# The fourth attention pair's last four chunks transposed two a turn, in a fused attention and two-MLP kernel

## The chip, the cores and the metric

The kernel runs on one core of a Trainium2 chip. The metric is the device time of one execution in microseconds. Three timed executions of the kernel before took 1118.45, 1120.15 and 1120.5 us; their median is 1120.15 us. One more execution was profiled, and all rows below come from it.

## The reference

```python
def _attn_ref(q, k, v, tau):                  # 4 batches, 8 heads, 576 rows, 64 wide
    scores = scale * np.matmul(q, k.transpose(0, 1, 3, 2))
    thresh = np.max(scores, axis=-1, keepdims=True) - tau
    scores = np.where(scores >= thresh, scores, -1000000000.0)
    scores = scores - np.max(scores, axis=-1, keepdims=True)
    attn = np.exp(scores)
    attn = attn / (np.sum(attn, axis=-1, keepdims=True) + 1e-09)
    return np.matmul(attn, v)

def _moe_ref(x, w_in, w_out, s, b):           # 2304 tokens, 512 -> 2048 -> 512
    r = np.maximum(x @ w_in, 0.0)
    return (s * (r * r) + b) @ w_out

def _moe2_ref(x, w_in, w_out):
    h = x @ w_in
    return (h * np.tanh(softplus(h))) @ w_out
...
```

Attention's output, 2304 tokens of 512, goes through the first MLP and then through the second.

## The kernel before

**Attention** goes by pairs of heads: 16 pairs, numbered from 0, four to a batch, so pair 3 is the fourth and completes the first batch. A pair has nine score tiles of 128 rows and nine chunks of 128 key columns. The generator `attention` runs in turns. Turn `k` writes out the scores of pair `k // 9`, tile `k % 9`: TensorE computes `S` (line 346), VectorE scales it into `ns` and takes its maximum (350), ScalarE takes the exponential `e` (358), VectorE masks and sums it (364), and GpSimd normalises it (374). The same turn writes out chunk `k - 7` (`LAG = 7`): `weights_t` transposes the chunk's five blocks into the PSUM tile `T` (387, 392), and ScalarE copies that to `te` (398). `T` has one buffer, so each transposing waits for the copy of the chunk before it. When chunk 6 of a pair has been copied, `products_v` multiplies chunks 1, 4 and 0 by v into `pv` (414, 417), 12 matmuls; after chunk 8 it does chunks 3 and 2, 8 matmuls (two chunks of 64 rows go in as one, and chunk `c` takes `te_c` and `te_(c+5)`). I call these the first and the second run of products. Then `split_x` puts `pv` into the two halves `xh` (ScalarE, 425) and `xl` (VectorE, 426). The scores and the transposes of q and k for later pairs (`tpq`, `tpk`) share the PSUM tile `S`; their copies are `hiq`, `hik` (284) and `loq`, `lok` (285).

**The first MLP** (`moe1`, line 516 is its matmul) takes a batch when the batch's four pairs have their `x`. `run` first advances attention alone, until pair 3 has its `x`; on the turns in `AHEAD` (15, 20, 24, 29, 33, 38, 42) it also takes a step of the loading and splitting of the MLP's weights (lines 62 to 79). From then on it advances attention and MLP in turn, by the nanoseconds that each `yield` names. A third generator, `combine`, prepares the second MLP's weights between them: ScalarE and VectorE operations of lines 105 to 145 on tiles `crawi`, `afi`, `chli`, and stores to `wsi` (147).

**The order** in which this is written out isn't the order on the engines. A scheduler places each instruction by its own model of when operands and buffers are ready; what was written out earlier goes first where several are ready, attention ahead of the MLP. `issue_after` binds one instruction behind another: the first transpose of a turn behind the run of products written out in that turn. Each engine then works its queue strictly in that order, SyncE's queue of DMAs too.

Of the kernel before, what the change touches and what calls it, by code (L numbers as in the profile page):

```python
# [19 lines left out]
class Fused:  # L20
# [131 lines left out]
    def combine_all(self):  # L152
# [3 lines left out]
        def load(i):  # L156
            if i < 16 and i not in raws:
                raws[i] = self.combine_load(*steps[i])

        for i, step in enumerate(steps):  # L160
            if i not in raws:
                load(i)
                yield
                yield
            yield from self.combine(*step, raws.pop(i), lambda: i + 1 != EARLY and load(i + 1))

# [263 lines left out]
    def attention(self):  # L430

        nc = self.nc
        self.turn = 0
        N = 9 * self.B * self.NP
        LAG = 7
        for n in "kq":
            self.load_raw(0, n)
        nc.sync.dma_start(self.tau_c, self.tau.partition_broadcast(P))  # L440
        nc.sync.dma_start(self.s_c, self.s.partition_broadcast(P))
        nc.sync.dma_start(self.b_c, self.b.partition_broadcast(P))
        for pr in range(2):
            self.load_raw(pr, "v")
        warm = self.pvp.tile([P, 1024], F32, tag="pv", name="warm")[:, :512]
        self.busy(warm[:, :256], 20)
        self.prep_first(lambda n: self.busy(warm[:, :256], 2 * n))
        fin = todo = None
        tes = {}
        for k in range(N + LAG + 2):  # L450
            pr, ti = divmod(k, 9)
            self.turn = k
            if k < N:
                nxt = self.scores(pr, ti)
                if k < 12:
                    self.busy(warm[:, :256], 3)
                if fin:
                    fin()
                fin = nxt
                yield 550  # L460
                if pr + 1 == self.B * self.NP and ti == 2:
                    self.load_raw(pr, "v")
                if pr + 1 < self.B * self.NP and ti in (1, 4):
                    self.prep_qk(pr + 1, "kq"[ti // 4])
                    if ti == 4 and pr >= 2:
                        with self.tc.issue_after(self.moved):
                            self.load_raw(pr, "v")
                    yield 500
            elif fin:
                fin()  # L470
                fin = None
            j = k - LAG
            run = None
            if todo:
                tp, tc, te = todo
                tes[tc] = te
                if tc == 6:
                    run = self.products_v(tp, (1, 4, 0), tes, True, False)
                    yield 1460
                elif tc == 8:  # L480
                    run = self.products_v(tp, (3, 2), tes, False, True)
                    yield 970
                    self.split_x(tp)
            todo = None
            if 0 <= j < N:
                prj, ci = divmod(j, 9)
                todo = prj, ci, self.weights_t(prj, ci, run)
                yield 550

    def acc(self, name):  # L490
# [297 lines left out]
    def run(self, ctx):  # L788
# [28 lines left out]
        while 3 not in self.x:  # L817
            next(att)
            if self.turn > done and self.turn in AHEAD:
                next(w1)  # L820
# [13 lines left out]
        def moes():  # L834
# [5 lines left out]
            for b in (1, 2):  # L840
                while 4 * b + 3 not in self.x:
                    yield 0
                for i, c in enumerate(self.moe1(b)):
                    while n * 256 < (2 + 12 * EARLY) * (i + 128 * (b - 1)):
                        next(comb, None)
                        n += 1
                    yield c
            while self.combined < EARLY:
                next(comb)
# [46 lines left out]


EARLY = 14
AHEAD = [15] + [9 * pr + ti for pr in (2, 3, 4) for ti in (2, 6)]
HALVES = [slice(0, 64), slice(64, 128)]  # L900

# [49 lines left out]
```

## Time and profile before

| | |
|---|---|
| timed executions, median (lowest, highest) | 1120.15 us (1118.45, 1120.5) |
| profiled execution, its own time | 1117.13 us |
| its span, first to last instruction | 1114.9 us |
| TensorE matmuls busy | 1073.3 us, 96% |
| weight loads busy | 1012.0 us, 91% |
| VectorE, ScalarE, GpSimd busy | 792.9, 624.9, 285.1 us |
| mean granted TensorE clock | 0.995 of full speed |

A row of the stretch view gives a stretch in us from the span's start, its length, each engine's busy time with the number of instructions, the granted clock, and the DMA engines' share and rate. In the timeline a row is a group of like instructions: start, duration, engine, line, operation, what is written and read; in brackets how long the engine stood idle before it, and what ended that.

### The profile page before, as it was taken

How to read it: one execution, taken by the hardware profiler on the slowest of the kernel's cores; microseconds unless marked ns; L12 is line 12 of the kernel's file. 1: busy time of each engine (PE TensorE's matmuls, PEld its weight loads, DVE VectorE, ACT ScalarE, POOL GpSimd, SP SyncE). 2: the span in 40 equal slices, each digit the busy share in tenths (PEclk: the TensorE clock that was granted, in tenths of full speed). 3: DMA queues.
4: the chain of work that ended last, by engine and by line, in shares of the span. 5: the costliest groups of instructions: out<-in, count | busy, mean ns of one | idle time of the engine just before them, and what ended most of it. 6: DMA issues, size and time to landing. Idle time of an engine off the chain costs nothing.

```text
span 1114.9 us, 21378 instructions
## 1 busy us (share of the span) xinstructions
PE 1073.3 (96%) x7964; PEld 1012.0 (91%) x7964; DVE 792.9 (71%) x1662; ACT 624.9 (56%) x1189; POOL 285.1 (26%) x354
## 2 busy tenths in 40 slices
PE   7987899999999999899999989999999999999998
PEld 6766789999899999879999879999999999999998
DVE  5989699998556777878757656735695468725782
ACT  5777687585486575577746667634453245413451
POOL 4556454355072351344515201100000000000000
PEclk9999999999999999999999999999999999999999
DMA  7577588785666879969855599968998999997783
GB/s 165 132 179 218 149 269 243 237 256 178 196 182 216 259 220 285 306 202 310 305 177 196 184 368 359 357 224 311 349 393 314 364 418 380 342 333 255 261 288 119
DMA packets 141590, 292.69 MB, mean 263 GB/s; under 512 B 52848, under 2 KB 78960, under 8 KB 133168
## 3 DMA queue, kind: packets, MB, share of 16 engines
q1 hardware_dynamic: 127104, 277.93, 74.0%
q10 hardware_dynamic: 14384, 13.40, 4.1%
q8 instruction: 63, 1.03, 0.4%
q14 instruction: 39, 0.32, 0.1%
HBM read 201.85 MB, written 66.58 MB: 241 GB/s over the span
## 4 chain that ended last, share of the span: by engine, by line
PE 70%; DVE 5%; DMA 5%; POOL 2%; issue 2%; ACT 1%; SPq 0%; ACTq 0%; DVEq 0%; POOLq 0%
PE o L761 16%; PE y L516 14%; PE h L516 12%; PE qY L627 7%; PE qX L627 5%; PE qV L627 4%; PE S L346 4%; PE pv L417 3%; PE T L387 3%; DMA wsi<-chli 2%; DMA w<-w 2%; POOL e L374 1%; DMA wso<-chlo 1%; PE pv L414 1%; DVE ns L350 1%
## 5 line engine op out<-in xcount | busy, mean ns | idle before, releaser
L761 PE MATMUL o<-wo,hl 128*128 128x256 f32 x1512 | 177.7, 279 | 0.0
L761 PEld LDWEIGHTS o<-wo,hl 128*128 128x128 f32 x1512 | 177.4, 188 | 0.0
L516 PE MATMUL h<-xh,w 128*128 128x288 f32 x768 | 164.6, 299 | 2.2 <-ACT xh L425 0.7
L516 PE MATMUL y<-gh,w 128*128 128x288 f32 x768 | 164.8, 299 | 1.3 <-DVE y L563 0.8
L374 POOL TENSOR_SCALAR e<-e,st 128x576 f32<-128x576 f32 x128 | 140.5, 1109 | 34.0 <-DVE st L369 24.7
L350 DVE TENSOR_SCALAR_CACHE_REDUCE ns<-S 128x576 f32<-128x576 f32 x144 | 108.0, 752 | 43.9 <-PE S L346 43.0
L358 ACT ACTIVATE e<-ns,st 128x576 f32<-128x576 f32 x128 | 98.9, 775 | 71.1 <-DVE ns L350 67.8
L364 DVE SCALAR_TENSOR_TENSOR e<-ns,st,e 128x576 f32<-128x576 f32 x128 | 114.1, 895 | 26.4 <-ACT e L358 22.9
L516 PEld LDWEIGHTS h<-xh,w 128*128 128x128 f32 x768 | 126.0, 188 | 3.7 <-ACT xh L425 1.2
L516 PEld LDWEIGHTS y<-gh,w 128*128 128x128 f32 x768 | 126.3, 188 | 2.5 <-DVE y L563 1.4
L398 ACT COPY te<-T 128x576 f32<-128x576 f32 x144 | 91.2, 633 | 50.2 <-PE T L392 45.1
L540 POOL TENSOR_TENSOR gl<-rr,gh 128x288 fp32r<-128x288 f32 x96 | 90.3, 952 | 108.9 <-ACT rr L539 107.8
L516 PE MATMUL h<-xl,w 128*128 128x288 f32 x384 | 113.7, 296 | 0.0
L516 PE MATMUL y<-gl,w 128*128 128x288 f32 x384 | 113.4, 295 | 0.0
L346 PE MATMUL S<-KH,Q 128*128 128x288 f32 x320 | 96.2, 318 | 15.7 <-DVE ns L350 7.3
L387 PE MATMUL T<-ident,e 128*128 128x128 f32 x576 | 90.9, 278 | 7.2 <-ACT te L398 5.0
L387 PEld LDWEIGHTS T<-ident,e 128*128 128x128 f32 x576 | 68.0, 142 | 24.2 <-issue 13.6
L346 PE MATMUL S<-KL,Q 128*128 128x288 f32 x320 | 89.9, 297 | 0.0
L627 PE MATMUL qY<-yc,wi 128*128 128x384 f32 x432 | 86.6, 337 | 1.3 <-DVE g L650 1.3
L417 PE MATMUL pv<-te,rawv 128*64 128x288 f32 x576 | 87.8, 423 | 0.0
L346 PEld LDWEIGHTS S<-KH,Q 128*128 128x128 f32 x320 | 60.6, 190 | 21.7 <-DVE ns L350 10.5
L627 PEld LDWEIGHTS qY<-yc,wi 128*128 128x128 f32 x432 | 75.6, 188 | 1.9 <-DVE g L650 1.9
(151 smaller groups left out, 2204.1 us busy)
## 6 DMA issues: line engine op xcount, KB each, us to landing
w<-w SPq DMA_DIRECT2D x96, 512.0 KB, 5.4
wo<-wso SPq DMA_DIRECT2D x42, 1024.0 KB, 7.1
wi<-wsi SPq DMA_DIRECT2D x23, 1024.0 KB, 8.2
wi<-wsi SPq DMA_DIRECT2D x25, 768.0 KB, 8.0
w<-wp SPq DMA_DIRECT2D x32, 512.0 KB, 4.7
wsi<-chli SPq DMA_DIRECT2D x24, 512.0 KB, 4.8
wso<-chlo SPq DMA_DIRECT2D x24, 512.0 KB, 7.1
ycd<-yp SPq DMA_DIRECT2D x14, 768.0 KB, 7.6
```

Source lines behind the costliest of these rows:

```text
L346: self.scored = nc.tensor.matmul(so, Q[:, c0:c0 + 128], kt[:, ks], start=(i == 0), stop=(i == len(terms) - 1)).ins
L350: nc.vector.tensor_scalar(ns.rearrange("p (h n) -> p h n", h=2), sv, -0.125, 3.0e38, op0=ALU.mult, op1=ALU.min, accum_out=nm[:, c1])
L358: nc.scalar.activation(e, ns, AF.Exp, bias=nm[:, c1], scale=-1.0)
L364: nc.vector.scalar_tensor_tensor(e, ns, nthr[:, c1], e, op0=ALU.is_le, op1=ALU.mult, accum_out=sm[:, c1])
L374: nc.gpsimd.tensor_scalar(t, t, rinv[:, j:j + 1], u[:, j:j + 1], op0=ALU.mult, op1=ALU.add)
L387: nc.tensor.transpose(T[:, i * 128:i * 128 + 128], self.es[pr, i, "pair"][:, o:o + 128], self.ident)
L398: nc.scalar.copy(te, T[:, :576])
L417: ins = self.nc.tensor.matmul(*args, **kw).ins
L516: nc.tensor.matmul(acc[:, :n], w[:, wl, c], rhs[c][xl][:, ts], start=(i == 0), stop=(i == 11))
L540: (nc.vector if b == 3 else nc.gpsimd).tensor_tensor(gl[:, ts], r2, gh[:, ts].bitcast(F32), op=ALU.subtract)
L627: self.nc.tensor.matmul(acc, a, b, start=(first and i == 0), stop=(i == n - 1), skip_group_check=True)
L761: nc.tensor.matmul(bank[p][t], hl[:, gl, j, ts], w[:, 2 * (q % 2) + j, wl], start=(old is None and q + j + k == 0), stop=(q + j + k == 6), ...
```

## The change

`due(k)` replaces the fixed lag. It gives chunk `k - 7` as before, except in four turns: turn 39 transposes chunks 32 and 33 (pair 3, chunks 5 and 6), turn 40 chunks 34 and 35 (chunks 7 and 8), turns 41 and 42 none. The runs of products hang on chunks 6 and 8 as before, so they are written out in turns 40 and 41 instead of 41 and 43. Only the first transposing of a turn is bound behind that turn's products. `SOLO = 0` selects the same runs as before for every pair. The `yield`s of the products now name 486 ns for each chunk (1458 and 972 instead of 1460 and 970).

```diff
-        fin = todo = None
-        tes = {}
+        fin, todo, tes = None, [], {}
+        soon = {39: (32, 33), 40: (34, 35), 41: (), 42: ()} if TWO else {}
+
+        def due(k):
+            return soon.get(k, (k - LAG,) if 0 <= k - LAG < N else ())
+
...
-            if todo:
-                tp, tc, te = todo
+            for tp, tc, te in todo:
                 tes[tc] = te
-                if tc == 6:
-                    run = self.products_v(tp, (1, 4, 0), tes, True, False)
-                    yield 1460
-                elif tc == 8:
-                    run = self.products_v(tp, (3, 2), tes, False, True)
-                    yield 970
+                for chunks in RUNS[tp < SOLO].get(tc, ()):
+                    run = self.products_v(tp, chunks, tes, chunks == RUNS[tp < SOLO][min(RUNS[tp < SOLO])][0], tc == 8)
+                    yield 486 * len(chunks)
+                if tc == 8:
                     self.split_x(tp)
-            todo = None
-            if 0 <= j < N:
+            todo = []
+            for j in due(k):
                 prj, ci = divmod(j, 9)
-                todo = prj, ci, self.weights_t(prj, ci, run)
+                todo.append((prj, ci, self.weights_t(prj, ci, run)))
+                run = None
                 yield 550
...
+SOLO = 0
+TWO = True
+RUNS = ({6: [(1, 4, 0)], 8: [(3, 2)]}, {5: [(0, 4)], 6: [(1,)], 7: [(2,)], 8: [(3,)]})
```

What the scheduler makes of it is shown at three places. In the rows, the figure behind a tile's name is its chunk or score tile, and the last figure a running number.

TensorE's queue at the first run of products of pair 3, before:

```order
L392 MATMUL T_6_1354<-ident,E_113 128x128
L346 MATMUL S_8_1463<-KH_120,Q_117 128x288
L346 MATMUL S_8_1463<-KL_122,Q_117 128x288
L346 MATMUL S_8_1463<-KH_120,Q_117 128x288
L346 MATMUL S_8_1463<-KL_122,Q_117 128x288
L414 MATMUL pv_1378<-te_6_1360,rawv_136 64x288
```

and now:

```order
L392 MATMUL T_6_1320<-ident,E_113 128x128
L346 MATMUL S_8_1463<-KH_120,Q_117 128x288
L346 MATMUL S_8_1463<-KL_122,Q_117 128x288
L346 MATMUL S_8_1463<-KH_120,Q_117 128x288
L346 MATMUL S_8_1463<-KL_122,Q_117 128x288
L414 MATMUL pv_1362<-te_6_1326,rawv_136 64x288
```

Nothing moved there; the run stands at the same row of the queue, and everything ahead of it on all five queues is in the old order.

TensorE's queue at the second run of products of pair 3 (`T_0` is the first chunk of pair 4), before:

```order
L346 MATMUL S_1_1508<-KL_129,Q_125 128x288
L414 MATMUL pv_1378<-te_8_1427,rawv_136 64x288
L417 MATMUL pv_1378<-te_3_1262,rawv_136 64x288
L417 MATMUL pv_1378<-te_8_1427,rawv_136 64x288
L417 MATMUL pv_1378<-te_3_1262,rawv_136 64x288
L417 MATMUL pv_1378<-te_7_1397,rawv_136 64x288
L417 MATMUL pv_1378<-te_2_1224,rawv_136 64x288
L417 MATMUL pv_1378<-te_7_1397,rawv_136 64x288
L417 MATMUL pv_1378<-te_2_1224,rawv_136 64x288
L387 MATMUL T_0_1451<-ident,e_0_1208 128x128
```

and now:

```order
L346 MATMUL S_1_1508<-KL_129,Q_125 128x288
L387 MATMUL T_0_1455<-ident,e_0_1208 128x128
L387 MATMUL T_0_1455<-ident,e_1_1234 128x128
L387 MATMUL T_0_1455<-ident,e_2_1272 128x128
L387 MATMUL T_0_1455<-ident,e_3_1309 128x128
L392 MATMUL T_0_1455<-ident,E_113 128x128
L414 MATMUL pv_1362<-te_8_1389,rawv_136 64x288
L417 MATMUL pv_1362<-te_3_1262,rawv_136 64x288
```

The five transposes of `T_0` moved from behind the run to ahead of it. Behind them, the next transposing `T_1` also moved ahead of the MLP's first two `h` matmuls on `xh`. On ScalarE the copy `te_0` moved ahead of `xh`.

VectorE's queue where the second batch's MLP ends and the third's is about to begin (`chli` is the weight combining, `y_3` the MLP's last sums), before:

```order
L145 TENSOR_TENSOR chli_5871<-chli_5871 128x2x256
L563 SCALAR_TENSOR_TENSOR y_3_4178<-y_3_3_0_6575,small,y_3_4178 128x288
L350 TENSOR_SCALAR ns_3_5754,st_5549<-S_3_5749 128x576
L353 TENSOR_SCALAR st_5549<-st_5549,small 128x1
L145 TENSOR_TENSOR chli_5991<-afi_5667,chli_5991 128x2x256
L563 SCALAR_TENSOR_TENSOR y_3_4178<-y_3_3_1_6613,small,y_3_4178 128x288
L364 SCALAR_TENSOR_TENSOR e_3_5757,st_5549<-ns_3_5754,st_5549,e_3_5757 128x576
L350 TENSOR_SCALAR ns_4_5797,st_5549<-S_4_5788 128x576
```

and now:

```order
L564 SCALAR_TENSOR_TENSOR y_2_4164<-y_3_2_1_6528,small,y_2_4164 128x288
L145 TENSOR_TENSOR chli_5973<-afi_5637,chli_5973 128x2x256
L350 TENSOR_SCALAR ns_3_5774,st_5587<-S_3_5769 128x576
L564 SCALAR_TENSOR_TENSOR y_3_4165<-y_3_3_0_6557,small,y_3_4165 128x288
L353 TENSOR_SCALAR st_5587<-st_5587,small 128x1
L364 SCALAR_TENSOR_TENSOR e_3_5777,st_5587<-ns_3_5774,st_5587,e_3_5777 128x576
L564 SCALAR_TENSOR_TENSOR y_3_4165<-y_3_3_1_6595,small,y_3_4165 128x288
L350 TENSOR_SCALAR ns_4_5841,st_5587<-S_4_5832 128x576
```

The last `chli` subtraction moved from behind `ns_3` to ahead of it. On TensorE the eight matmuls of `S_4` there moved from behind the first nine `h` matmuls of the third batch to ahead of them.

Elsewhere TensorE's queue is in the old order up to the second batch's MLP but for three swaps of one or two matmuls. From there to about the end of the third batch's MLP, some 2,150 matmuls, attention's steps stand up to 12 MLP matmuls earlier, for one pair later, and on SyncE's, ScalarE's and VectorE's queues the combining's steps stand a few places off. Behind that the queues agree again but for a few neighbours.

## Rows read from the trace of the kernel before

**Rows 1.** Page, busy time of each engine over the span:

```profile
PE 1073.3 (96%) x7964; PEld 1012.0 (91%) x7964; DVE 792.9 (71%) x1662; ACT 624.9 (56%) x1189; POOL 285.1 (26%) x354
```

**Rows 2.** Stretches of the span; the columns are in the first line:

```profile
core 0: us, PE busy (x) PEld busy (x) DVE busy (x) ACT busy (x) POOL busy (x), PEclk, DMA share, GB/s
0.00:140.00 140.00, 115.87 (x829) 95.85 (x830) 112.95 (x288) 93.56 (x175) 72.40 (x104) 0.98 0.66 170
...
316.00:640.00 324.00, 317.38 (x2425) 293.45 (x2425) 236.11 (x566) 205.96 (x414) 127.79 (x145) 0.99 0.76 240
...
112.62:133.08 20.46, 17.41 (x122) 12.84 (x120) 11.49 (x34) 10.44 (x18) 8.85 (x11) 0.92 0.38 119
```

**Rows 3.** Timeline of TensorE around the two runs of products of pair 3:

```profile
118.33 0.46 PE L414 MATMUL pv<-te,rawv 128*64 128x288 f32 x1 [2.01 <-ACT te L398]
...
126.71 0.46 PE L414 MATMUL pv<-te,rawv 128*64 128x288 f32 x1 [0.59 <-ACT te L398]
...
128.81 0.66 PE L387 MATMUL T<-ident,e 128*128 128x128 f32 x4
...
129.41 0.33 PE L276 MATMUL tpk<-ident,rawk 128*128 128x64 f32 x2
...
130.16 0.51 PE L516 MATMUL h<-xh,wp 128*128 128x288 f32 x2
130.51 0.60 PE L387 MATMUL T<-ident,e 128*128 128x128 f32 x4
...
130.97 0.38 PE L516 MATMUL h<-xl,wp 128*128 128x288 f32 x1
...
131.95 0.66 PE L387 MATMUL T<-ident,e 128*128 128x128 f32 x4 [0.20 <-ACT te L398]
```

**Rows 4.** Timeline of ScalarE in the same stretch:

```profile
117.10 0.65 ACT L71 ACTIVATE wraw<-wraw 128x512 f32<-128x512 f32 x1 [2.22 <-DMA wraw<-in_moe_w_out_dram]
...
126.04 0.62 ACT L398 COPY te<-T 128x576 f32<-128x576 f32 x1
...
128.92 0.64 ACT L425 CAST xh<-pv 128x576 fp32r<-128x576 f32 x1 [1.12 <-PE pv L417]
...
130.39 0.69 ACT L284 CAST hik<-tpk 128x640 fp32r<-128x640 f32 x1
131.26 0.64 ACT L398 COPY te<-T 128x576 f32<-128x576 f32 x1 [0.17 <-PE T L392]
```

**Rows 5.** Timelines of VectorE and GpSimd in the same stretch:

```profile
129.59 0.76 DVE L426 TENSOR_TENSOR xl<-pv,xh 128x576 fp32r<-128x576 f32 x1 [0.47 <-ACT xh L425]
...
121.54 3.23 POOL L374 TENSOR_SCALAR e<-e,st 128x576 f32<-128x576 f32 x4 [0.27 <-DVE st L369]
```

**Rows 6.** Stretches after three long waits of TensorE, columns as in rows 2:

```profile
118.00:124.00 6.00, 5.67 (x32) 3.23 (x33) 3.30 (x10) 1.11 (x3) 2.69 (x5) 0.72 0.28 91
473.00:479.00 6.00, 6.00 (x35) 3.44 (x35) 1.80 (x5) 0.86 (x2) 2.23 (x3) 0.72 0.92 231
653.00:659.00 6.00, 4.09 (x28) 2.77 (x29) 5.90 (x13) 2.70 (x5) 0.00 (x0) 1.00 0.87 302
```

**Rows 7.** Waits of TensorE between 316 and 640 us: total us, times, longest:

```profile
PE S L346 <- DVE loq L285: 1.6, 1, 1.6
PE T L387 <- POOL e L374: 1.5, 1, 1.5
...
PE h L516 <- DVE y L563: 0.6, 1, 0.6
```

**Rows 8.** Timelines of VectorE, ScalarE and TensorE where the third batch's MLP begins:

```profile
463.68 0.75 DVE L350 TENSOR_SCALAR_CACHE_REDUCE ns<-S 128x576 f32<-128x576 f32 x1
...
467.31 0.69 DVE L145 TENSOR_TENSOR chli<-afi,chli 128x512 fp32r<-128x512 f32 x1 [2.62 <-ACT chli L143]
...
466.65 0.62 ACT L143 CAST chli<-afi 128x512 fp32r<-128x512 f32 x1 [3.02 <-DMA wsi<-chli]
...
469.89 0.44 PE L276 MATMUL tpq<-ident,rawq 128*128 128x64 f32 x2
```

More of the change, by code (lines that the diff above doesn't have):

```diff
@@ L471, in attention @@
                 fin = None
-            j = k - LAG
             run = None
-            if todo:
-                tp, tc, te = todo
+            for tp, tc, te in todo:
                 tes[tc] = te
-                if tc == 6:
-                    run = self.products_v(tp, (1, 4, 0), tes, True, False)
-                    yield 1460
-                elif tc == 8:
-                    run = self.products_v(tp, (3, 2), tes, False, True)
-                    yield 970
+                for chunks in RUNS[tp < SOLO].get(tc, ()):
+                    run = self.products_v(tp, chunks, tes, chunks == RUNS[tp < SOLO][min(RUNS[tp < SOLO])][0], tc == 8)
+                    yield 486 * len(chunks)
+                if tc == 8:
                     self.split_x(tp)
-            todo = None
-            if 0 <= j < N:
+            todo = []
+            for j in due(k):
                 prj, ci = divmod(j, 9)
-                todo = prj, ci, self.weights_t(prj, ci, run)
+                todo.append((prj, ci, self.weights_t(prj, ci, run)))
+                run = None
                 yield 550
```

## The prediction

> **What bounds the kernel now.** I read the page's busy times first. TensorE's matmuls fill 1073.3 of 1114.9 us [rows 1], so what an edit can win is TensorE's idle time and the time that it runs at a lower clock; the number of matmuls stays the same here. The stretch view then says where that time is [rows 2]. In the first 140 us TensorE is busy for 115.87 us, so 24.1 of its 41.6 idle us lie there, with attention alone at work for most of it. Between 316 and 640 us, where attention and the MLP of the second and third batch are mixed, it idles 324 - 317.38 = 6.6 us. The place of the edit is the stretch from 112.62 to 133.08 us, the end of the attention-only part: TensorE idles 20.46 - 17.41 = 3.05 us there.
>
> The timeline of that stretch names the waits [rows 3]. The first run of products of pair 3 waits 2.01 us for `te_6`, the second 0.59 us for `te_8`, and a later transposing, `T_2` of pair 4, waits 0.20 us for `te_1`. ScalarE's rows tell why `te_6` is late: it stands behind a scaling of weights that itself waits 2.22 us for a load [rows 4]. The clock is the last view. In the six microseconds that begin with the first run it averages 0.72 of full speed [rows 6], so some of them ran at 1.2 GHz and 6 x 0.28 = 1.7 us were lost.
>
> **The change part by part.** What is written out two turns sooner isn't placed sooner. The scheduler goes by readiness, and the chain that decides is one buffer of `T`: transposing, copy, next transposing. The first run stands at its old row of TensorE's queue with nothing reordered ahead of it on any queue. The wait of 2.01 us, the load behind it and the low clock stay; I cost this part at 0. The extra transposing per turn costs no instruction either. The `yield`s of 1458 and 972 ns for 1460 and 970 are 0.
>
> What does move is `T_0` of pair 4. Turns 41 and 42 write out no transposing, so nothing binds `T_0` behind the second run any more, and its five transposes go ahead of it. This doesn't fill the wait of 0.59 us: `T_0` needs the buffer that the same copy `te_8` empties (ScalarE, from 126.04 for 0.62 us, so to 126.66) [rows 4]. Its other operand has long been ready, GpSimd having normalised the last four `e` by 121.54 + 3.23 = 124.77 [rows 5]. So `T_0` starts where the run started, at 126.71. The pitch of a transposing is 129.41 - 128.81 = 0.60 us and that of the run 128.81 - 126.71 = 2.10 us [rows 3], so the run goes from 127.31 to 129.41, and `tpk` then starts at 129.41, exactly where it did. Up to there the sum is 0: two neighbours have changed places.
>
> Who is queued behind it: `xh` needs the end of the run and slips by 0.60, from 128.92 to about 129.52, ending at 130.16; `xl` slips from 129.59 to 130.19 and ends at 130.95 [rows 4, 5]. The old queue would have asked for `xh` at 130.16 and for `xl` at 130.97 [rows 3]. In the new one `T_1` comes first (130.16, for 130.97 - 130.51 = 0.46 us to 130.62), so the two `h` matmuls on `xh` start at about 130.62, with 0.46 us to spare, and those on `xl` at about 130.97 after their 130.51 - 130.16 = 0.35 us, when `xl` is just there. The slip is covered; without `T_1` ahead of it, it would cost up to 0.60.
>
> The gain is at `T_2`. It waits for the copy `te_1`, which began at 131.26, 0.17 us after ScalarE had come free [rows 4]. With `T_1` 0.35 us sooner the copy is held by `hik` alone, whose input `tpk` hasn't moved; it can begin at 131.26 - 0.17 = 131.09. So `T_2` starts about 0.17 to 0.20 us sooner, and what comes behind is TensorE's own work. I take **0.2 us gained**. The ends are 0.6 lost (the whole slip of `xh` shows) and 0.8 gained (0.59 + 0.20, both waits gone).
>
> The second part is what follows from the shift in what is written out when. In the second and third batch, attention's steps stand up to 12 MLP matmuls from their old place, and the weight combining a few places off on three other queues, its loads and stores on SyncE's among them. No row of before shows these orders. From above the gain is bounded by all that TensorE lost there: 6.6 us idle and 6 x 0.28 = 1.7 us of clock after 473 us [rows 2, 6], 8.3 together. From below I have one priced place (the slower rival). Since TensorE is busy for 98% of the stretch, a step that comes 12 matmuls sooner or later mostly changes places with other work of TensorE. The value I take is 0.
>
> **Sum**: 1114.9 - 0.2 = 1114.7 us of span, with 1117.13 - 1114.9 = 2.2 us around it 1116.9 us of profiled execution. The profiled execution is 3.0 us below the median of the timed ones, so on their scale it is 1120.15 - 0.2, **1119.9 us**. About 0.2%, 2.2 us, is what a measurement of this kernel can tell from no change.
>
> **The rivals.**
>
> *The products really come sooner* (the change does what its words say). If pair 3's `x` came early enough for the first MLP's matmuls to fill the idle time of the stretch, 3.05 us [rows 2] would go: 1117.1 us. Against it stands the order, in which the first run hasn't moved at all and the second moved back. Chance 0.05.
>
> *Faster by the reshuffle.* The largest waits between 316 and 640 us are single events: 1.6 us of `S` for `loq`, 1.5 us of a transposing for GpSimd's `e`, 0.6 us of `h` for a sum of VectorE [rows 7]. The low clock after 473 us follows the first of them [rows 6, 8]. If the new order breaks the 0.6 and the 1.5 us, or breaks the 0.6 and escapes the low clock (1.7), that gives 2.1 to 2.3, with the 0.2 some 2.5 us: 1117.7 us. For it: `S_4` now stands ahead of nine `h` matmuls, so a sum of VectorE has 9 matmuls longer. Against it: the chain `tpq`, `hiq`, `loq`, `S_5`, which makes the 1.6 us, is in the old order. Chance 0.20.
>
> *Slower: a score behind a store.* Where the third batch begins, `ns_3` on VectorE now stands behind the last `chli` subtraction. That one waited for ScalarE's copy, and the copy 3.02 us for a store to `wsi` to land; the subtraction ran from 467.31 for 0.69 us, while `ns_3` ahead of it ran at 463.68 [rows 8]. `ns_3` holds the one buffer of `S`, and `S_4` now comes nine matmuls sooner. If the store lands as late as before, `ns_3` runs from 468.00 to 468.75. Behind it come eight matmuls of `S_4` and 18 of `h`, at 317.38 / 2425 = 0.13 us each [rows 2], 3.4 us, so `tpq` starts at 472.2 instead of 469.89: 2.3 us lost. With the 0.2 that is 1122.2 us, and 1123.9 if the clock falls after a wait that is longer than before, once more by 1.7; I give 1123.0. It decides from the landing: `ns_3` has to end by 469.89 - 3.4 = 466.5 to cost nothing, so the subtraction by 465.7 and the store must land some 2 us sooner than at 466.65. Against it: the same combining now stands several steps sooner on VectorE, so the store is also issued sooner. Other queues where combining and attention have changed places can do the same. Chance 0.18.
>
> *The clock falls elsewhere.* After waits of 2.01 and 1.6 us the clock averaged 0.72 over six microseconds, but it stayed at 1.00 around 653 us [rows 3, 6, 7], where TensorE was idle for 6.00 - 4.09 = 1.9 of six microseconds too. So a wait alone doesn't decide. If the 0.2 us takes away one fall or adds one, the time is 1118.2 or 1121.6 us, both within 0.2%. The Trainium skill, "TensorE: Matmul & The Clock Gate", section "What's actually happening", says that the activity is judged in windows that run free of the kernel; by that rule a shift of a fraction of a microsecond can do this without any wait changing, and no run here shows it yet. Chance 0.10.
>
> **How the numbers follow.** The forecast itself has 0.47: 1119.9 us, by its own bounds 1119.4 to 1120.8. With the clock's 0.10, within 0.2% has 0.57. Faster by over 0.2% has 0.20 + 0.05 = 0.25, slower 0.18. The range for 8 in 10 reaches from the reshuffle's gain with something over it, 1116.8, to the slower rival with most of its clock fall, 1123.4.
>
> **What would show it right or wrong.** In the changed kernel's trace the first run of products should still wait about 2.0 us for its `te` near 118 us, with the clock near 0.72 behind it. Five transposes should stand after the 0.6 us wait near 126.7, then the eight products, then `tpk` near 129.4, and the wait before the third transposing behind it should be shorter than 0.20 us. If the first run starts sooner than 118.0, the part costed at 0 is wrong. If `h` on `xh` or `xl` waits near 130.6 or 131.0, the cover failed. TensorE's idle time from 316 to 640 us decides between the forecast (6 to 7 us) and the reshuffle's two sides; the idle time before `S_4` near 466 us tests the slower one. A time outside 1117.9 to 1122.4 us would make the forecast wrong.

## The result, and the profile after

| | before | after |
|---|---|---|
| median of 6 runs each, us | 1119.11 (1116.11 to 1120.5) | 1124.2 (1122.07 to 1125.76) |
| ratio, 95% interval | | 1.0056 (1.0029 to 1.0083) |
| profiled execution, us | 1117.13 | 1124.27 |
| its span, us | 1114.9 | 1122.2 |

The change makes the kernel slower by 0.56%, some 6 us, where 1119.9 us and "within 0.2%" were forecast. The measured 1124.2 lies above the range's end of 1123.4. TensorE does the same work, as the page's first part says beside [rows 1]. Most of the time is in what lies between its matmuls: TensorE idles 1122.2 - 1074.0 = 48.2 us instead of 41.6, which is 6.6 of the 7.3 us between the two spans.

```profile
PE 1074.0 (96%) x7964; PEld 1012.8 (90%) x7964; DVE 800.3 (71%) x1662; ACT 622.3 (55%) x1189; POOL 283.1 (25%) x354
```

I first read the place of the edit, in TensorE's timeline of the changed kernel (start, us, engine, line, operation, and in brackets the wait before it). It answers [rows 3]:

```profile
116.70 0.46 PE L414 MATMUL pv<-te,rawv 128*64 128x288 f32 x1 [2.93 <-ACT te L398]
...
125.17 0.63 PE L387 MATMUL T<-ident,e 128*128 128x128 f32 x4 [0.69 <-ACT te L398]
...
125.83 0.46 PE L414 MATMUL pv<-te,rawv 128*64 128x288 f32 x1
...
127.93 0.44 PE L276 MATMUL tpk<-ident,rawk 128*128 128x64 f32 x2
...
130.30 0.66 PE L387 MATMUL T<-ident,e 128*128 128x128 f32 x4
```

The first run still waits. `T_0` now goes first, after a wait of 0.69 us where the run waited 0.59; the second run follows 0.66 us later, and `tpk` stands 2.76 us behind `T_0`. `T_2` at 130.30 has no wait any more, and no `h` matmul waits for `xh` or `xl`. The loss isn't here. It begins after 316 us. The stretch view answers [rows 2], and for the two stretches around 640 us I put before's (first pair) beside after's (second pair):

```profile
316.00:640.00 324.00, 312.50 (x2383) 289.25 (x2382) 235.88 (x562) 201.07 (x407) 123.44 (x143) 0.99 0.76 239
```

```profile
640.00:660.00 20.00, 16.43 (x123) 13.27 (x123) 13.61 (x29) 9.34 (x17) 0.00 (x0) 1.00 0.99 363
660.00:740.00 80.00, 79.86 (x603) 79.62 (x603) 48.34 (x91) 50.36 (x119) 9.19 (x8) 1.00 0.95 355
```

```profile
640.00:660.00 20.00, 18.80 (x143) 15.71 (x142) 7.64 (x16) 7.06 (x12) 0.00 (x0) 1.00 0.63 215
660.00:740.00 80.00, 76.66 (x567) 76.43 (x567) 57.46 (x103) 53.56 (x126) 10.37 (x8) 0.98 0.99 376
```

The first number behind a stretch is TensorE's busy time, the third from the end its clock, the last two are the busy share of the DMA engines and GB/s. Between 316 and 640 us TensorE now idles 324 - 312.50 = 11.5 us instead of 6.6. From 640 to 660 the DMA engines are busy 0.63 of the time instead of 0.99, so 0.36 x 20 = 7.2 us of transfers are missing there, and from 660 to 740 they are full and TensorE idles 3.3 us. The view of waits names what is new (total us, times, longest). `r` is the ReLU of the first MLP's `h`, `gh` and `gl` are the two halves of its square, `w` is a block of the first MLP's weights:

```profile
PE h L517 <- DMA w<-w: 3.3, 1, 3.3
PE h L517 <- ACT r L538: 2.2, 2, 1.8
PE y L517 <- POOL gl L541: 2.0, 1, 2.0
```

Their places, in TensorE's timeline:

```profile
548.90 0.40 PE L517 MATMUL h<-xh,w 128*128 128x288 f32 x1 [1.79 <-ACT r L538]
...
634.94 0.40 PE L517 MATMUL y<-gl,w 128*128 128x288 f32 x1 [1.97 <-POOL gl L541]
...
723.89 0.40 PE L517 MATMUL h<-xh,w 128*128 128x288 f32 x1 [3.34 <-DMA w<-w]
```

Two of these waits cost more than themselves in this execution, because the clock falls behind them, as it did in [rows 6]:

```profile
634.90:641.00 6.10, 6.06 (x36) 6.05 (x37) 3.78 (x7) 2.65 (x4) 0.74 (x1) 0.72 0.80 255
...
720.50:723.90 3.40, 0.06 (x2) 0.01 (x1) 3.40 (x6) 3.28 (x6) 0.00 (x0) 1.00 1.03 419
723.90:727.00 3.10, 3.10 (x17) 3.10 (x18) 3.10 (x4) 1.55 (x4) 0.00 (x0) 0.69 1.02 414
727.00:730.00 3.00, 3.00 (x19) 3.00 (x19) 0.64 (x2) 1.53 (x5) 0.00 (x0) 0.76 1.06 378
730.00:733.00 3.00, 3.00 (x25) 3.00 (x24) 0.92 (x2) 2.20 (x7) 0.00 (x0) 1.00 0.98 361
```

0.72, 0.69 and 0.76 are means of stretches in which the clock ran partly at 1.2 GHz. Behind the wait at 724 that is 3.1 x 0.31 + 3.0 x 0.24 = 1.7 us lost, so this wait costs about 3.3 + 1.7 = 5.0 us. Behind the wait for `gl` at 635 it is 6.1 x 0.28 = 1.7 us too; but e9 below, with the same wait of 1.96 us there, kept a clock of 1.00 from 634 to 642 us, so that fall comes in some executions and not in others.

Two losses of before are gone: the wait of `pv` for `te` at 653.57 (2.23 us), and 1.7 us of clock after 473 us [rows 6]. The second is no gain of the change: some executions of either order have it, as the last section shows.

### The profile page after: what moved, and what is told of

Its sections match the earlier page's. It is cut to its first block, busy times and chain, and to the rows that moved or that the text cites. A ratio compares the mean times of both kernels' runs of the same rounds, so it can differ in the third digit from the quotient of the medians.

```text
span 1122.2 us, 21389 instructions
## 1 busy us (share of the span) xinstructions
PE 1074.0 (96%) x7964; PEld 1012.8 (90%) x7964; DVE 800.3 (71%) x1662; ACT 622.3 (55%) x1189; POOL 283.1 (25%) x354
## 5 line engine op out<-in xcount | busy, mean ns | idle before, releaser
L517 PE MATMUL h<-xh,w 128*128 128x288 f32 x768 | 166.9, 301 | 7.0 <-DMA w<-w 3.3
```

Of the source, the lines that this page charges most:

```text
L517: nc.tensor.matmul(acc[:, :n], w[:, wl, c], rhs[c][xl][:, ts], start=(i == 0), stop=(i == 11))
```

## Experiments: the edit's own place, or the reshuffle

Theory R: the edit does no harm where it is made. But pair 3's `x` is set a turn or two sooner, so that a score's and a transposing's `yield` (550 each) now fall into the account `a_done` of the interleave loop. That shifts attention against the MLP by 1100, and the reshuffle of batches 2 and 3 that follows costs the time. Rival L: the edit's own place costs it. Each ratio below is to runs of the kernel before on the same chip, with its 95% interval. Two ratios from different chips can be compared only as far as both intervals allow.

**e1**, the edit with the pace undone. Batches 2 and 3 get before's order on every engine:

```diff
-            if a_on and (not m_on or (a_done - 5000.0) / a_left <= m_done / m_left):
+            if a_on and (not m_on or (a_done - 6100.0) / a_left <= m_done / m_left):
...
-                    yield 486 * len(chunks)
+                    yield {3: 1460, 2: 970}[len(chunks)]
```

> The changed kernel with the interleave loop's constant raised from 5000 to 6100 and the products' yields set back to 1460 and 970: batches 2 and 3 have the instructions of before on every engine, and the edit itself (two transposed chunks a turn, the products two turns sooner) stays. Theory R (the reshuffle of batches 2 and 3 makes the loss): back to about 1118.9 us, 0.2 below before (ratio 0.9998, between 0.998 and 1.001), PE idle 6 to 7 us between 316 and 640, no wait of 3 us for w near 724. Rival L (the edit's own place makes it, by what it leaves to later stages): about 1124, ratio 1.004 to 1.006.

Measured: **1.0009 (0.9991 to 1.0027)**, TensorE's idle time from 316 to 640 us 324 - 316.46 = 7.5 us, no wait for `w` near 724.

**e2**, the reshuffle without the edit, on the kernel before:

```diff
-            if a_on and (not m_on or (a_done - 5000.0) / a_left <= m_done / m_left):
+            if a_on and (not m_on or (a_done - 3900.0) / a_left <= m_done / m_left):
...
-                    yield 1460
+                    yield 1458
...
-                    yield 970
+                    yield 972
```

> The kernel before with nothing but the interleave loop's constant lowered from 5000 to 3900 and the yields 1458 and 972: batches 2 and 3 take the order of the changed kernel, pair 4's chunks stay one a turn. Theory R: 1124 to 1125 us, ratio 1.004 to 1.008, PE idle 11 to 12 us between 316 and 640 and a wait of about 3 us for w near 724. Rival L: 1119, ratio within 0.999 to 1.001.

Measured: **1.0049 (1.0031 to 1.0066)**. Its waits are the changed kernel's:

```profile
PE h L516 <- DMA w<-w: 3.0, 1, 3.0
PE y L516 <- POOL gl L540: 2.0, 1, 2.0
PE h L516 <- ACT r L537: 1.5, 2, 1.1
```

R holds, L falls: the reshuffle alone makes the loss, the edit alone none that can be measured.

**e3** and **e4** cut the reshuffle in two, by the batch whose MLP is being handed out (`self.mb`, set in `moes`). e3 has before's order up to some 590 us, e4 from there on:

```diff
+                self.mb = b
                 for i, c in enumerate(self.moe1(b)):
...
+        self.mb = 0
...
-            if a_on and (not m_on or (a_done - 5000.0) / a_left <= m_done / m_left):
+            if a_on and (not m_on or (a_done - (6100.0 if self.mb < 2 else 5000.0)) / a_left <= m_done / m_left):
```

(e4 has the two numbers the other way round.)

> The changed kernel with the constant at 6100 until the third batch's MLP begins and 5000 from there: the order of before up to about 590 us, and the changed kernel's from there to the end of the attention. If the loss is made behind 590 us (the wait of 1.97 us for gl at 635, its clock fall, the 3.34 us for w at 724, less the 2.23 us before 653 that goes): about 3 to 4 us over before, ratio 1.0025 to 1.004. If it is made ahead of that place: 1119, ratio within 0.999 to 1.001.

> The changed kernel with the constant at 5000 until the third batch's MLP begins and 6100 from there: the changed kernel's order from 316 to about 570 us, the order of before behind it. If the loss is made there (the waits of 0.88, 0.52, 0.46 for r and te, 1.24 for POOL's e and 1.79 for r at 549, less the clock fall near 473): 2 to 4 us over before, ratio 1.002 to 1.0035; if all of it is made behind: 1119, ratio within 0.999 to 1.001. Theory R wants the excess of this run and of the third-batch run to add up to 5 to 6 us.

Measured: e3 **1.0037 (1.0020 to 1.0054)**, with the wait of 1.99 us for `gl` and 3.26 us for `w`; e4 **1.0019 (1.0001 to 1.0036)**, with the waits for `r` and `te` and only 0.23 us for `w`. The excesses, 0.37 and 0.19%, add up to the whole 0.56%, each known to about 0.17%. So about two thirds of the loss, as far as these intervals tell, is made behind 590 us, by what e3 has and e4 hasn't.

## Experiments: the late part

Why do the DMA engines run empty at 640 us? ScalarE's timeline of the changed kernel shows the third batch's four `yo` (the first MLP's output) with nothing but copies between them, each waiting for a sum of VectorE, and the next scaling of raw weights (`crawo`, L105) behind the last:

```profile
637.36 0.78 ACT L570 ACTIVATE yo<-y,small 128x576 f32<-128x576 f32 x1 [0.39 <-DVE y L564]
...
642.49 0.78 ACT L570 ACTIVATE yo<-y,small 128x576 f32<-128x576 f32 x1 [1.52 <-DVE y L564]
...
646.26 0.78 ACT L570 ACTIVATE yo<-y,small 128x576 f32<-128x576 f32 x1 [1.55 <-DVE y L564]
...
653.15 0.78 ACT L570 ACTIVATE yo<-y,small 128x576 f32<-128x576 f32 x1 [1.45 <-DVE y L564]
...
654.88 0.67 ACT L105 ACTIVATE crawo<-crawo 128x512 f32<-128x512 f32 x1
```

SyncE, in order too, issues its `yd` stores there and no `wso` store between 637.23 and 659.62. In before, four `wso` stores leave in that time:

```profile
643.54 0.33 SPq L147 DMA_DIRECT2D wso<-chlo  x1
...
645.38 1.31 SPq L147 DMA_DIRECT2D wso<-chlo  x2
...
652.63 0.37 SPq L147 DMA_DIRECT2D wso<-chlo  x1
```

Theory D: what wasn't moved then is moved later, ahead of the `w` that TensorE needs at 720.55, and makes that load late. SyncE in the changed kernel:

```profile
705.94 0.37 SPq L634 DMA_DIRECT2D wi<-wsi  x1
706.58 3.52 SPq L147 DMA_DIRECT2D wso<-chlo  x4
711.02 0.33 SPq L634 DMA_DIRECT2D wi<-wsi  x1
711.77 0.47 SPq L147 DMA_DIRECT2D wso<-chlo  x1
713.04 7.86 SPq L509 DMA_DIRECT2D w<-w  x5
```

The DMA view of 700 to 724 us gives 10.0 us from issue to landing for `w` (median of 7), against 5.5 over the whole page. In before it is 9.2 us in the same stretch and no matmul waits, so the slow landing alone doesn't make the wait. Two edits of the changed kernel test theory D from both ends.

**e5** puts the combining forward again, so that it stands between the `yo`:

```diff
-                    while n * 256 < (2 + 12 * EARLY) * (i + 128 * (b - 1)):
+                    while (n - 24 * (b == 2 and i >= 64)) * 256 < (2 + 12 * EARLY) * (i + 128 * (b - 1)) and self.combined < EARLY:
```

> The changed kernel with the combining of the second MoE's weights asked for up to 24 steps sooner from the 64th step of the third batch's MLP on (never past the 14 of EARLY): on TensorE the order stays but for 19 matmuls at the very end of the third batch and later; on ScalarE and SyncE the crawo and chlo steps and the wso stores stand again between the yo steps and yd stores instead of behind them. Theory D (in the changed kernel the DMA queue runs empty between 640 and 657 because these steps stand behind the yo of the third batch, and the 3.3 us for w at 724 pay for it): DMA share of 640:660 back above 0.9, the wait for w gone or under 0.5 us, 3 us less than the changed kernel, ratio to before 1.002 to 1.004. Rival Q (the queue has the same bytes to move and the wait only goes elsewhere, to wi or to w of the last batch): the ratio stays 1.005 to 1.006. The 2 us wait for gl at 635 stays under both.

Measured: **1.0035 (1.0018 to 1.0052)**. The queue is full again and the wait for `w` is gone:

```profile
640.00:660.00 20.00, 16.84 (x126) 13.52 (x125) 12.62 (x27) 9.65 (x17) 0.00 (x0) 1.00 0.94 328
660.00:740.00 80.00, 80.00 (x607) 80.00 (x606) 48.41 (x91) 50.62 (x118) 9.66 (x8) 1.00 0.94 353
```

The ratio is 0.21% below the changed kernel's, which is less than the two intervals together can tell (0.32%): the trace shows the wait gone, the time doesn't show what that is worth. Part is paid where the combining went: `T` waits 0.92 us for `te` at 651.78, and `h` 1.79 us for `xh` at 657.61 instead of 0.74.

**e9** leaves the order alone, and only holds the first loads of the second MLP's weights until `w_1_2_3` has been issued. These are the three `wi`, 1.8 MB; two of them, 1.5 MB, were issued ahead of the five `w` above.

```diff
-            nc.sync.dma_start(w.bitcast(F32), self.w1s[key])
+            d = nc.sync.dma_start(w.bitcast(F32), self.w1s[key])
+            if b == 3 and key == (1, 2, 3):
+                self.held = d.ins
...
-        w0 = self.weights_in(0, 0, self.hl, "hl", ((6, 5, 1), (2, 4, 7), (3,)))
+        with self.tc.issue_after(self.held):
+            w0 = self.weights_in(0, 0, self.hl, "hl", ((6, 5, 1), (2, 4, 7), (3,)))
```

> The changed kernel with the first three loads of the second MoE's weights (wi, 2 MB) held in SyncE's queue until the last batch's w_1_2_3 is issued; nothing else moves on TensorE before the second MoE. Theory D (w near 724 waits because the queue of transfers started its last stretch late and is full from 660 on): 2 MB less ahead of it is about 5 us at 384 GB/s, so the wait of 3.3 us goes, and the ratio to before falls to 1.002 to 1.004, unless the first product of the second MoE then waits for wi. Rival: that wait appears, at least 2 us before qX, and the ratio stays at 1.005 to 1.006.

Measured: **1.0018 (0.9998 to 1.0037)**. The queue runs as empty at 640 as before the mend, but TensorE doesn't wait:

```profile
640.00:660.00 20.00, 18.81 (x143) 15.71 (x142) 7.73 (x16) 7.42 (x12) 0.00 (x0) 1.00 0.67 236
660.00:740.00 80.00, 80.00 (x606) 80.00 (x606) 58.94 (x107) 52.60 (x126) 10.57 (x8) 1.00 1.01 382
```

From 1.0056 to 1.0018 is 0.38% or 4.3 us, against 5.0 counted for the wait with its clock; the two intervals together leave it uncertain by 0.33%, so the gain is only just clear of the noise. That agrees with e3's 0.37%, though e3's part has the wait for `gl` too. The `w` issued from 700 to 724 us land after 6.8 us here. No wait for `wi` appeared before the second MLP's first product.

**e6** takes the wait for `gl` at 635 away, by computing the last four `gl` of the third batch on VectorE; **e7** does that in e5's kernel:

```diff
-                    (nc.vector if b == 3 else nc.gpsimd).tensor_tensor(gl[:, ts], r2, gh[:, ts].bitcast(F32), op=ALU.subtract)
+                    (nc.vector if b == 3 or (b, qf, fc) in ((2, 3, 2), (2, 3, 3)) else nc.gpsimd).tensor_tensor(gl[:, ts], r2, gh[:, ts].bitcast(F32), op=ALU.subtract)
```

> The changed kernel with the four gl differences of the third batch's last two hidden chunks on VectorE instead of GpSimd. Theory P (gl stands on GpSimd behind four scalings of e that take 1.37 us each instead of 0.81): the wait of y for gl at 635 falls from 2.0 to under 0.8 us, ratio to before 1.003 to 1.005, with the wait for w near 724 still there. Rival V (VectorE's own queue, which holds the combining there, is as late): the wait only changes its name, ratio 1.005 to 1.007.

> Both of the former edits in the changed kernel. If D and P are both right, what is left is the second batch's part of the loss: ratio 1.000 to 1.003, near the 1.0019 of the run that had the reshuffle only until the third batch. If the two pay on the same stretch (the queue is late by what TensorE lost and so on), less than the sum: 1.003 to 1.005.

Measured: e6 **1.0050 (1.0029 to 1.0071)**, e7 **1.0030 (1.0010 to 1.0051)**. In e6 the wait near 635 fell to 0.30 us, but the one for `w` grew:

```profile
724.60 0.61 PE L517 MATMUL h<-xh,w 128*128 128x288 f32 x1 [4.47 <-DMA w<-w]
```

TensorE comes 2 us sooner only to wait 1.1 us longer, as if the queue were the bound there. In e7, without that wait, the gain over e5 is 0.05%, less than these intervals can tell. So the 2 us at 635 were real in the trace, and no gain from taking them away can be measured in the time.

## Experiments: the second batch's part

With `wi` held 0.18% are left, and e4 has 0.19%. Their waits for `r` and `te` have a common look on ScalarE, here in the changed kernel near 438 and 547 us:

```profile
437.96 0.68 ACT L105 ACTIVATE crawi<-crawi 128x512 f32<-128x512 f32 x1 [2.08 <-DMA crawi<-in_moe_w_in_dram]
438.54 0.61 ACT L398 COPY te<-T 128x576 f32<-128x576 f32 x1
...
546.70 0.68 ACT L105 ACTIVATE crawo<-crawo 128x512 f32<-128x512 f32 x1 [1.79 <-DMA crawo<-in_moe_w_out_dram]
547.28 0.60 ACT L143 CAST chlo<-chlo 128x512 fp32r<-128x512 f32 x1
547.78 0.77 ACT L358 ACTIVATE e<-ns,st 128x576 f32<-128x576 f32 x1
548.46 0.39 ACT L538 ACTIVATE r<-h 128x288 f32<-128x288 f32 x1
```

A scaling of raw weights waits for its load, and `te` or `r` behind it waits with it. **e13** puts these loads ahead on SyncE by a higher priority, TensorE's and GpSimd's order unchanged; **e14** does the same in e9's kernel:

```diff
-            self.nc.sync.dma_start(raw.rearrange("p (c f) w -> p c (f w)", c=src.shape[1]), src)
+            with self.tc.high_priority(offset=1000):
+                self.nc.sync.dma_start(raw.rearrange("p (c f) w -> p c (f w)", c=src.shape[1]), src)
```

> The changed kernel with the transfers of the second MoE's raw weights (crawi, crawo) at a higher priority: four of them stand two to five rows sooner on SyncE, nothing moves on TensorE or GpSimd, and three rows on ScalarE. Theory C (ScalarE's scaling of crawi and crawo, which waits 2.1 us for its transfer at 438 and 1.8 at 547, keeps te and r back, and TensorE waits 0.5 and 1.8 us for them): those waits of TensorE go under 0.3 us each, 1 to 2 us less than the changed kernel, ratio 1.004 to 1.005. Rival S (the second batch's part is in the order of TensorE's own work, or the transfers moved ahead only delay the queries and keys that they pass): ratio 1.0055 or more, the waits still there or turned into waits of S for loq.

> Both transfers' mends in the changed kernel: the raw weights ahead, and wi held behind w_1_2_3. wi held alone gave 1.0018. Theory C: 1.000 to 1.001. Rival S: 1.0018 or more.

Measured: e13 **1.0074 (1.0049 to 1.0100)**, e14 **1.0016 (1.0001 to 1.0031)**. The wait for `r` near 548 is gone in both, but the one for `te` near 441 is there (1.06 and 0.39 us), because ScalarE still waits 2.63 us for `crawi` in e13. e14 gains nothing on e9 that can be measured. Both times miss what theory C forecast, and the wait for `r` went without the time following. What makes the second batch's 0.2% stays open. It is about the size of one interval.

## Experiments: other draws of the same pace

The prediction put a reshuffle's worth at nothing. Three more constants, on the kernel before, ask what a reshuffle is worth as such; **e8** (6100), **e12** (4450) and **e16** (5550) change that one number:

```diff
-            if a_on and (not m_on or (a_done - 5000.0) / a_left <= m_done / m_left):
+            if a_on and (not m_on or (a_done - 6100.0) / a_left <= m_done / m_left):
```

> The kernel before with the interleave loop's constant raised from 5000 to 6100, the same shift of 1100 to the other side: attention is handed out sooner against the MLP, and the order changes from PE row 727 on. It tells what a reshuffle of this size is worth in itself. If the order of before lies at a favourable point and any shift loses: ratio 1.002 to 1.008. If a shift is as likely to gain (what the prediction assumed when it put the reshuffle at nothing): 0.996 to 1.002.

> The kernel before with the constant at 4450, half of the shift that the change makes. A second draw of what a reshuffle costs: the full shift gave 1.0049, the same shift to the other side 1.0004. If the cost grows with the shift: 1.002 to 1.003. If it depends on which steps fall on which, with no order in it: anywhere from 0.998 to 1.006, with its own set of waits.

> The kernel before with the constant at 5550. One more draw of a reshuffle: so far 3900 gave 1.0049, 4450 0.9973, 6100 1.0004. If a shift costs as a rule: 1.002 to 1.005. If its price is a matter of which steps fall together: anywhere from 0.997 to 1.005, and the waits on TensorE (those for r behind the raw weights, for gl at 635, for w at 720) say which.

| constant | ratio to before (95%) | longest waits of TensorE behind 316 us in its profile |
|---|---|---|
| 3900 (e2, the changed kernel's pace) | 1.0049 (1.0031 to 1.0066) | `w` 2.99, `gl` 1.95, `loq` 1.64 |
| 4450 (e12) | 0.9973 (0.9954 to 0.9993) | `te` 1.17, `ns` 0.86, none for `w` |
| 5000 (before) | 1 | `te` 2.23, `loq` 1.64, `e` 1.47 |
| 5550 (e16) | 1.0056 (1.0032 to 1.0079) | `w` 4.53, `r` 2.53 |
| 6100 (e8) | 1.0004 (0.9987 to 1.0021) | `w` 3.27, `loq` 1.95, `y` 1.38 |

There is no trend in the constant, and the kernel before isn't the best of them. Each order draws its own set of waits (each list is from one execution), and the spread is -0.3 to +0.6%. Three of the four other orders have the wait for `w`, so **e17** and **e18** hold `wi` as e9 did, in the orders of 5550 and 6100:

> The kernel before with the constant at 5550 (alone: 1.0056, with 4.5 us of wait for w in its profile) and wi held behind w_1_2_3. Theory D: that wait goes and 3 to 4.5 us with it, ratio 1.0015 to 1.003. Rival: its loss is in the waits for r at 360 (2.5 us) and 445, and the queue's wait only covered it: 1.004 or more.

> The kernel before with the constant at 6100 (alone: 1.0004, with 3.3 us of wait for w in its profile) and wi held behind w_1_2_3. Theory D: the wait goes, 2.5 to 3.5 us less than alone, ratio 0.997 to 0.998, below both kernels. Rival: 0.9995 to 1.001.

Measured: e17 **0.9973 (0.9960 to 0.9987)** from 1.0056, e18 **0.9951 (0.9935 to 0.9966)** from 1.0004. Holding `wi` carries to orders it wasn't found on. e18 is the fastest version here, 0.5% under the kernel before and 1% under the changed one. Both gains are larger than was expected. In e18 the wait for `w` shrank to 1.30 us, so 0.53% or 5.9 us is more than the 2.0 us of it and a clock fall of 1.6 (0.98 from 660 to 740 us in e8 and e16, 1.00 in e18 and e17); e17's 9 us is more than its 4.5 and 1.6 too. The intervals of the two pairs leave the gains uncertain by 2.6 and 3.0 us, which about covers the rest. The same order also draws other waits in another execution: e16's 2.53 us for `r` at 359 us isn't in e17, which has 3.52 us for `te` at 537 instead.

The other half of theory D, the queue running empty at 640 us, does not carry. In e8 the DMA engines are full there, and `w` is awaited for 3.27 us all the same:

```profile
640.00:660.00 20.00, 19.00 (x142) 17.50 (x143) 13.90 (x31) 13.26 (x32) 0.00 (x0) 1.00 1.01 384
```

So the empty stretch is how the changed kernel's order came to this wait, and other orders come to it in another way. What e9, e17 and e18 share is that `wi` no longer stands in the full queue ahead of the late `w`.

Three other mends, on the way. **e10** lets the raw weights of the first MLP (`wraw`), whose landing ScalarE awaits ahead of `te_6` [rows 4], be loaded sooner; **e11** joins this with 6100, `wi` held and the combining forward; **e15** joins 4450 with e13's priority.

```diff
-        if self.s2p:
+        if self.s2p and self.turn > 24:
+            nc.sync.dma_start(dst, src)
+        elif self.s2p:
             with self.tc.issue_after(self.moved):
                 nc.sync.dma_start(dst, src)
```

> The kernel before, with the raw weights that are loaded from turn 25 on no longer held behind the prepared keys' transfers (moved): wraw of in_moe_w_out stands about 20 rows sooner on SyncE. Batches 2 and 3 keep before's order. If ScalarE's scaling of wraw is what holds te_6 at pair 3's first product run (2.0 us of wait there in before, 0.2 to 5.2 in the profiles of the other runs, and a granted clock of 0.72 behind it): the wait goes under 0.3 us and the clock stays at 1.00, 2 to 3.5 us less, ratio 0.997 to 0.998. Rival: the transfers share the queue and te_6 or the prepared keys come as late: 0.999 to 1.001.

> The kernel before with the constant 6100 instead of 5000 (that order had no wait for gl at 635 and none before the last products at 653, but one of 3.3 us for w), the wraw loads sooner, wi held behind w_1_2_3, and the combining up to 24 steps sooner late in the third batch. If the reasons hold, the 3.3 us and the 2 to 3.5 us both go: ratio 0.994 to 0.997. If the waits only change places: 0.999 to 1.001.

> The kernel before with the constant at 4450 (alone: 0.9973) and the raw weights' transfers ahead. If that order's gain is real and its waits for r and lok hang on the same transfers: 0.995 to 0.998. If 0.9973 was a lucky draw of the runs: 0.9985 to 1.000.

Measured: e10 **1.0025 (1.0006 to 1.0044)**, e11 **0.9987 (0.9969 to 1.0005)**, e15 **0.9977 (0.9958 to 0.9996)**. In e10 the wait before the first run is gone, but one that stands 10 us ahead of it, 1.88 us in before, has grown to 3.86. TensorE's and ScalarE's timelines there:

```profile
107.41 0.66 PE L389 MATMUL T<-ident,e 128*128 128x128 f32 x4 [3.86 <-ACT te L400]
```

```profile
106.13 0.69 ACT L286 CAST hiq<-tpq 128x640 fp32r<-128x640 f32 x1 [2.98 <-DMA KH<-hik]
106.72 0.65 ACT L400 COPY te<-T 128x576 f32<-128x576 f32 x1
```

With the load ahead of it, the transfer of the prepared keys (`KH`) lands 7.3 us after issue instead of 3.3, `hiq` waits for that, and `te` stands behind `hiq`: the wait has changed its place and its cause. e11 against e18 points the same way, 0.9987 against 0.9951; the two differ by this mend and by the combining put forward, which moves a few rows on ScalarE there.

## Why the prediction failed, step by step

- **The products aren't placed sooner, cost 0**: right. The first run kept its row and waited 2.93 us, with the clock at 0.72 from 117 to 123 us.
- **`T_0` ahead of the second run, 0.2 us gained**: right in mechanism, too large in size. `T_0` took the run's place, `tpk` came 2.76 us behind it (0.60 + 2.10 were forecast), the slip of `xh` and `xl` was covered, the wait of `T_2` is gone, and from `T_0` to `T_2` are 130.30 - 125.17 = 5.13 us instead of 131.95 - 126.71 = 5.24. That is 0.11 us gained, and the wait ahead of `T_0`, 0.69 us instead of 0.59, takes 0.10 of it back. e1, which has only this, can't be told from before.
- **The reshuffle, "the value I take is 0"**: this step failed. e2, which has the reshuffle alone, is slower by 0.49%, 5.5 us. The step was wrong in three ways. First, its ground, that steps only change places with other work of TensorE, looks at TensorE's own queue alone. What cost here is which step stands ahead of which on ScalarE, GpSimd and SyncE, where a step that waits holds all behind it. Second, the stretch was drawn by TensorE's order, and the largest cost fell outside it: the order on ScalarE and SyncE changed at 640 us, and TensorE paid at 724, in the last batch's MLP. Third, the bounds were not symmetric. The gain was bounded by all idle time (8.3 us), the loss by one priced place (2.3 us). A wait that isn't in the trace can't be read from it, so the honest lower bound was of the upper one's size. The five pace constants, -0.3 to +0.6%, are what such a term is worth here.
- **The rival "a score behind a store"**: the right sign and nearly the right time (1123.0 against 1124.2), by luck, since the mechanism was another. Near 466 us, its place, no wait stands in the changed kernel. Its last sentence, that other queues where combining and attention have changed places can do the same, was the cause; it should have had the chance, not the place. Slower deserved far more than 0.18.
- **The rival "faster by the reshuffle"**: its 0.6 us at 468 did go and the clock stayed up after 473 in this execution, but `e` at 497 still took 1.24 us, and what was won there is less than what the new waits took.
- **The clock**: it was named as a rival that moves the time by less than 0.2%. It came as a part of other costs, 1.7 us on top of the 3.3 us at 724 and, in the profiled execution, 1.7 us on top of the 2.0 at 635.

## What to carry to other kernels

An edit that shifts what one generator hands out can reorder a whole kernel: compare the order of every engine, DMA queues included, to the last row that differs, and give a reshuffle a spread (here -0.3 to +0.6%) instead of a zero. In a late stretch where the DMA engines are full, hold back what is needed last; here that was worth 0.4 to 0.8% in three different orders, each known to about 0.3%. Before moving a load ahead, look whose transfer it then delays.

## What was not expected of the hardware

*The clock falls or not after the same wait.* 13 of the profiles have the same 1.64 us wait of `S` for `loq` near 473 us, in two orders. In four the next transposing that waits comes 7.0 us later, in nine 5.3 us. Here e1 (first) and e3 (second), which have before's order there:

```profile
474.81 0.40 PE L346 MATMUL S<-KH,Q 128*128 128x288 f32 x1 [1.64 <-DVE loq L285]
...
481.83 0.66 PE L387 MATMUL T<-ident,e 128*128 128x128 f32 x4 [0.26 <-ACT te L398]
```

```profile
468.76 0.40 PE L346 MATMUL S<-KH,Q 128*128 128x288 f32 x1 [1.64 <-DVE loq L285]
...
474.09 0.66 PE L387 MATMUL T<-ident,e 128*128 128x128 f32 x4 [0.26 <-ACT te L398]
```

The 1.7 us between them are the clock fall of [rows 6]. The Trainium skill, "TensorE: Matmul & The Clock Gate", section "What's actually happening", says that the activity is judged in windows that run free of the kernel; by that rule the same wait may or may not bring the clock down, and these rows agree.

*The same load lands at different times.* The wait before the first run, 2.01 us in [rows 3], is one draw: in the 18 profiles that have it, it lies between 0.20 (e3, e8) and 5.16 us (e1), with the same order around it. Its 5 us are 0.4% of the time, and e1's profiled execution, the one with 5.16 us, took 1122.46 us, 7 us over the median of e1's runs. No run changed this wait alone, so what it costs at the end of the kernel is argued; a profile taken once shows one value of it.

*VectorE and GpSimd slow each other.* The four scalings of `e` ahead of the late `gl` took 5.47 us in the changed kernel instead of 3.25 in before; the 3.23 of [rows 5] are four of the same. The changed kernel's rows, and the one of before:

```profile
628.66 5.47 POOL L374 TENSOR_SCALAR e<-e,st 128x576 f32<-128x576 f32 x4
634.10 1.54 POOL L541 TENSOR_TENSOR gl<-rr,gh 128x288 fp32r<-128x288 f32 x2
```

```profile
623.77 3.25 POOL L374 TENSOR_SCALAR e<-e,st 128x576 f32<-128x576 f32 x4
```

VectorE combines weights in those microseconds; in before it sat idle beside the same scalings from 623.77 on. The other way round, a step of the combining on VectorE (`afo` of `crawo` and `afo`, line 108) took 1.33 us at 628.87 in before, beside a `gl` of GpSimd, and 0.69 us at 637.69 in the changed kernel, with GpSimd idle. The Trainium skill, "SBUF — State Buffer", section "Who interferes with whom", says that the ports which the two engines share are an exclusive lock, and that a VectorE instruction with two inputs in SBUF contends with a GpSimd instruction that reads SBUF. The 2.2 us agree with it. No run here took VectorE's work away from under these scalings, so it is argued from the overlap, not shown by an experiment.
